# Reading integer phases in order and writing the table in strides: ScalarE's absolute values and sines in an S4D kernel

## The chip, the cores and the metric

The kernel runs on one core of a Trainium2 chip. The metric is the device time of one execution in microseconds (us), the median of several. A profiled execution leaves a trace, which gives the start and the end of each instruction on each engine. TensorE (PE) multiplies matrices, and its weight loads (PEld) are listed by themselves; VectorE (DVE) and ScalarE (ACT) work element by element; GpSimd (POOL) does next to nothing here; SyncE (SP) issues the DMAs.

## The reference

Two layers are computed and laid side by side. Layer A is a Fourier mixing of 2048 x 512 by DFT matrices. Layer B is a diagonal state space convolution: for each of 512 channels d, a kernel of 2048 taps is a sum over 128 states n of exponentials of complex rates, and the input is convolved with it.

```python
dt = jnp.exp(log_dt)
A = -jnp.exp(log_A_real) + 1j * A_imag
C = (C_real + 1j * C_imag) * dt[:, None]
P = jnp.exp((A * dt[:, None])[:, :, None] * pos[None, None, :])
K = 2.0 * jnp.einsum("dn,dnl->dl", C, P).real
...
y = jnp.fft.irfft(jnp.fft.rfft(u_t, L2) * jnp.fft.rfft(K, L2)[None], L2)[:, :, :L]
return y + u * D_skip[None, None, :]
```

The change lies in how the powers P are made: magnitude times cosine and sine of a phase.

## The kernel before, in words

A tap position is split into a coarse and a fine part, so that a tap is a product of two small complex tables, summed over the 128 states by TensorE. The states lie on the partitions. The channels are worked in 16 rounds of CHUNK = 32. In each round two tables are made:

- `t2`, [128, 32 channels d, 2 halves h, 2 parts c (real, imaginary), 32 positions l], of which positions 0 to 19 of each half come from phases. There are two of these tables, used in turn.
- `t1`, [128, 32 channels d, 2 parts c, 32 positions l], also with two buffers.

The phases are 32-bit integers, a full turn being 2^32, so that additions wrap by themselves. `phases2` and `phases1` (VectorE, line 977, from seeds that ScalarE copies in at lines 991, 992 and 1006) build them by doubling in `p2` [128, 40 positions, 32 channels] and `p1` [128, 32 positions, 32 channels]: position is the outer axis and channel the inner one. The tables have it the other way round, channel outside and position inside.

`sines` fills a table from its phases with three ScalarE instructions: the absolute value of the phases into the real part (line 1022), the sine of the phases into the imaginary part (line 1024), and then, in place over the real part, the sine of a quarter turn less the absolute value, which is the cosine (line 1026). The first two have 40 x 32 = 1280 elements on each partition for `t2` and 32 x 32 = 1024 for `t1`; each runs 16 times at each size. Once the sine into the imaginary part is done, the phase buffer may be written again (`p2s`, `p1s`: one buffer of each).

Behind `sines`, `magnitudes2` (product at line 1067) and `magnitudes1` (line 1088) multiply the tables by magnitudes that VectorE grows in `mag`, with the channel outside and the position inside; their seeds are written by ScalarE at lines 1059, 1060 and 1081, one float for each channel. `squares` (lines 1109 to 1120) makes further even positions of `t2` by squaring. `taps` (line 1151) multiplies `t1` by `t2` on TensorE, line 1156 copies the taps out, and line 1177 starts the Fourier transform of the taps. The rest of layer B (lines 1188 to 1411) and layer A (lines 253 to 612) run on the same engines in between.

The order of the instructions on each engine is laid down by a small planner in the program: each step is a generator that names an engine and an estimated duration before it issues its instruction, and `Plan.run` always takes the step that could start first. For the three steps of `sines` the estimate is `act(n) + 0.15` with `n` the product of the table view's extents, and `act(cols)` is `0.09 + cols * 0.00085`. Nothing in the planner knows strides. Memory and results are guarded by semaphores and events (`t1s`, `t2s`, `raw1_ev`, `raw2_ev`).

Of the kernel before, what the change touches and what calls it, by code (L numbers as in the profile page):

```python
# [12 lines left out]
AF = mybir.ActivationFunctionType  # L13
# [8 lines left out]
TWO_PI = 6.283185  # L22
LN2_HI = 0.693359375
LN2_LO = 0.693147180559945309 - LN2_HI
TURN = 2.0 ** 32
# [163 lines left out]
def act(cols):  # L189
    return 0.09 + cols * 0.00085  # L190
# [491 lines left out]
class Ssm:  # L682
# [334 lines left out]
    def sines(self, re, im, p, sign):  # L1017


        a, n = self.nc.scalar, math.prod(re.shape[1:])  # L1020
        yield "act", act(n) + 0.15
        a.activation(re, p, AF.Abs)  # L1022
        yield "act", act(n) + 0.15
        a.activation(im, p, AF.Sin, scale=sign * TWO_PI / TURN)  # L1024
        yield "act", act(n) + 0.15
        a.activation(re, re, AF.Sin, scale=-TWO_PI / TURN, bias=self.halfpi)  # L1026

    def sines2(self, n):
        yield self.t2s
        t, p = self.t2[n % 2], self.p2.rearrange("p (h l) d -> p d h l", h=2)  # L1030
        yield from self.sines(t[:, :, :, 0, :20], t[:, :, :, 1, :20], p, 1.0)
        self.plan.put(self.p2s)
        self.plan.set(self.raw2_ev[n])

    def sines1(self, n):
        yield self.t1s
        t = self.t1[n] = self.tab.tile([128, CHUNK, 2, 32], F32, name="t1", bufs=2)
        yield from self.sines(t[:, :, 0], t[:, :, 1], self.p1.rearrange("p m d -> p d m"), -1.0)
        self.plan.put(self.p1s)
        self.plan.set(self.raw1_ev[n])  # L1040

# [462 lines left out]
```

## Time and profile before

| | us |
|---|---|
| median of 3 runs | 607.92 (607.63 to 609.17) |
| the profiled execution | 607.69 |
| its span, first to last instruction | 605.8 |
| ScalarE busy | 424.0 (70% of the span) |
| TensorE matmuls busy | 430.5 (71%) |
| VectorE busy | 391.3 (65%) |
| line 1022, 32 instructions | 71.2 busy, 2230 ns each |
| line 1024, 32 instructions | 70.5 busy, 2203 ns each |
| line 1026, 32 instructions | 39.6 busy, 1247 ns each |

A row of a group names the line, the engine, the operation, what is written from what, the shape (partitions x elements on each, type) and the count; then busy us in total and the mean ns of one; then the idle time of the engine just before those instructions, with what ended it. A row of the waits reads: who waited, for whom, us in total, how many times, the longest. Of the 605.8 us, the chain that ended last can be followed back only through the last store, so the argument goes by stretches of time and by the waits instead.

### The profile page before, as it was taken

To read this page: it belongs to the slowest core of one execution; us is meant where nothing else is said; L and a number is where in the kernel's file an instruction comes from. 1 tells how busy PE (TensorE), PEld (TensorE's weight loads), DVE (VectorE), ACT (ScalarE), POOL (GpSimd) and SP (SyncE) were. 2 spreads that over 40 slices of the span, in tenths; PEclk is the share of its full clock that TensorE was granted. 3 is DMA by queue.
4 is the path that set the end of the run, shared out by engine and by line. 5 is a ranking of instruction groups with operands and counts; after the bars stand their busy time and mean duration, and the time that the engine had idled before them with its cause. 6 is when DMAs were issued, how large, how long until landed. Compare 5 with 4: busy or idle time off the path is not lost. (4 is left out here: it accounts for less than half of the span.)

```text
span 605.8 us, 13828 instructions
## 1 busy us (share of the span) xinstructions
PE 430.5 (71%) x5602; PEld 208.0 (34%) x5634; DVE 391.3 (65%) x843; ACT 424.0 (70%) x662; POOL 10.9 (2%) x25
## 2 busy tenths in 40 slices
PE   4678923196886967738885969798894887777542
PEld 3122201043332333333332443244243344445532
DVE  4996988656696757969976566589694563233110
ACT  2247488999979698886699697789948973434420
POOL 0000000000010001000001000000000000000000
PEclk7899965698997979959797979799997898788796
DMA  8979874184324692866486776284318137599893
GB/s 318 359 232 311 304 267 140 67 313 149 92 79 138 174 293 67 240 196 206 125 274 208 173 206 204 69 216 143 106 32 214 36 124 209 167 248 243 241 230 84
DMA packets 138837, 113.52 MB, mean 187 GB/s; under 512 B 64401, under 2 KB 108817, under 8 KB 138513
## 3 DMA queue, kind: packets, MB, share of 16 engines
q1 hardware_dynamic: 138048, 111.41, 60.8%
q10 hardware_dynamic: 720, 1.18, 0.5%
q8 instruction: 46, 0.75, 0.5%
q14 instruction: 23, 0.18, 0.1%
HBM read 78.09 MB, written 34.47 MB: 186 GB/s over the span
## 5 line engine op out<-in xcount | busy, mean ns | idle before, releaser
L587 PE MATMUL f<-p,w 128*128 128x512 f32 x128 | 73.8, 661 | 19.8 <-ACT y L612 18.7
L1022 ACT ACTIVATE t<-phase 128x1280 f32<-128x1280 int32 (+1 forms) x32 | 71.2, 2230 | 11.8 <-DVE phase L977 7.4
L1024 ACT ACTIVATE t<-phase 128x1280 f32<-128x1280 int32 (+1 forms) x32 | 70.5, 2203 | 0.1
L1067 DVE TENSOR_TENSOR t<-t,mag 128x2560 f32<-128x2560 f32 x16 | 45.2, 2824 | 36.8 <-ACT t L1026 36.8
L1088 DVE TENSOR_TENSOR t<-t,mag 128x2048 f32<-128x2048 f32 x16 | 36.6, 2290 | 49.7 <-ACT t L1026 49.7
L1046 DVE TENSOR_TENSOR mag<-mag,seeds 128x32 f32<-128x32 f32 (+5 forms) x176 | 61.9, 361 | 2.9 <-ACT mag L1059 2.4
L1151 PE MATMUL taps<-t,t 128*32 128x64 f32 x2048 | 38.4, 242 | 25.5 <-DVE t L1088 24.4
L977 DVE CUSTOM_DVE_ANT_0 phase<-seeds,phase 128x512 uint16<-128x512 uint16 (+4 forms) x128 | 52.8, 417 | 0.5
L1151 PEld LDWEIGHTS taps<-t,t 128*32 128x32 f32 x2048 | 35.6, 125 | 35.6 <-DVE t L1088 13.3
L1238 PE MATMUL f<-big,ib 64*128 64x512 f32 x64 | 21.8, 783 | 34.9 <-ACT big L1247 34.9
L514 PE MATMUL f<-base,es 128*128 128x512 f32 x64 | 38.3, 683 | 10.6 <-ACT xi L273 10.4
L587 PEld LDWEIGHTS f<-p,w 128*128 128x128 f32 x128 | 24.4, 204 | 46.6 <-ACT y L612 23.9
L416 DVE CUSTOM_DVE_ANT_1 rest<-slots,base 128x1024 bf16<-128x1024 f32 (+1 forms) x27 | 36.7, 1358 | 4.6 <-PE third L520 2.4
L1026 ACT ACTIVATE t<-t,halfpi 128x1280 f32<-128x1280 f32 (+1 forms) x32 | 39.6, 1247 | 0.0
L514 PE MATMUL f<-base,ec 128*128 128x512 f32 x64 | 35.9, 643 | 0.6 <-ACT low L567 0.6
L1319 PE MATMUL f<-big,w 64*32 64x256 f32 (+1 forms) x768 | 25.8, 392 | 14.4 <-ACT p L548 5.7
L1177 PE MATMUL f<-ks,f1k 32*128 32x512 f32 x128 | 25.8, 673 | 9.1 <-POOL ks L1166 7.2
L517 PE MATMUL f<-rest,xi 128*128 128x512 bf16 x89 | 27.8, 412 | 6.3 <-DVE small L416 3.3
L517 PE MATMUL f<-rest,xr 128*128 128x512 bf16 x85 | 25.0, 380 | 6.3 <-DVE small L416 5.8
L1335 ACT ACTIVATE big<-f 128x1024 f32<-128x1024 f32 x24 | 23.7, 1010 | 6.9 <-PE f L1319 4.6
L517 PEld LDWEIGHTS <-xr 128*128 128x128 bf16 (+1 forms) x144 | 13.5, 94 | 38.8 <-issue 31.3
L520 PE MATMUL third<-rest,small 128*1 128x512 bf16 x96 | 26.4, 384 | 0.0
(222 smaller groups left out, 766.0 us busy)
## 6 DMA issues: line engine op xcount, KB each, us to landing
slots<-in_sT SPq DMA_DIRECT2D x93, 256.0 KB, 4.6
xu<-big SPq DMA_DIRECT2D x16, 512.0 KB, 4.6
xk<-big SPq DMA_DIRECT2D x32, 256.0 KB, 4.5
base<-in_sT SPq DMA_DIRECT2D x31, 256.0 KB, 4.6
big<-xu SPq DMA_DIRECT2D x20, 256.0 KB, 4.5
big<-xk SPq DMA_DIRECT2D x20, 256.0 KB, 4.8
zs<-mid SPq DMA_DIRECT2D x20, 256.0 KB, 3.0
big<-zs SPq DMA_DIRECT2D x10, 512.0 KB, 6.1
```

Of the source, the lines that this page charges most:

```text
L416: return v.tensor_tensor_reduce(rest[:, lo:hi:step], raw[:, lo:hi:step], base[:, None, :].to_broadcast([128, n, DM]), 1.0, 0.0, op, OP.max ...
L514: nc.tensor.matmul(out, x[:, cols], base, start=k == 0, stop=False)
L517: nc.tensor.matmul(out, still[:, cols], rest[:, h], start=False, stop=k == 3 and h == 2)
L587: nc.tensor.matmul(ps, self.w[k][:, cols], self.p[t, c][:, d], start=k == 0, stop=False)
L977: self.nc.vector.tensor_tensor(p[:, to:to + m], p[:, of:of + m], seed[:, None, :].to_broadcast([128, m, CHUNK]), op=OP.add)
L1022: a.activation(re, p, AF.Abs)
L1024: a.activation(im, p, AF.Sin, scale=sign * TWO_PI / TURN)
L1026: a.activation(re, re, AF.Sin, scale=-TWO_PI / TURN, bias=self.halfpi)
L1046: self.nc.vector.tensor_tensor(p[:, :, to:to + m], p[:, :, of:of + m], seed[:, :, None].to_broadcast([128, CHUNK, m]), op=OP.mult)
L1067: v.tensor_tensor(t, t, p.rearrange("p d (h l) -> p (d h) l", h=2)[:, :, None, :].to_broadcast([128, 2 * CHUNK, 2, 20]), op=OP.mult)
L1088: v.tensor_tensor(t, t, p[:, :, None, :].to_broadcast([128, CHUNK, 2, 32]), op=OP.mult)
L1151: nc.tensor.matmul(ps[32 * j:32 * j + 32, i], t1[:, d, c], t2[:, d, :, c], start=c == 0, stop=c == 1, tile_position=(0, 32 * j))
```

## The change

The two instructions that read phases now walk over the elements in the order in which the phases lie: position outside, channel inside. The read goes through neighbours; the table is addressed through a view with its axes turned, so that each element is written one channel's distance from the last, 128 floats for `t2` and 64 for `t1`. The cosine's instruction keeps the old walk. The values are the same, at the same places.

```diff
         a, n = self.nc.scalar, math.prod(re.shape[1:])
+
+        def turned(x):
+            return x.rearrange("p d h l -> p h l d" if len(x.shape) == 4 else "p d l -> p l d")
         yield "act", act(n) + 0.15
-        a.activation(re, p, AF.Abs)
+        a.activation(turned(re), p, AF.Abs)
         yield "act", act(n) + 0.15
-        a.activation(im, p, AF.Sin, scale=sign * TWO_PI / TURN)
+        a.activation(turned(im), p, AF.Sin, scale=sign * TWO_PI / TURN)
         yield "act", act(n) + 0.15
         a.activation(re, re, AF.Sin, scale=-TWO_PI / TURN, bias=self.halfpi)

     def sines2(self, n):
         yield self.t2s
-        t, p = self.t2[n % 2], self.p2.rearrange("p (h l) d -> p d h l", h=2)
+        t, p = self.t2[n % 2], self.p2.rearrange("p (h l) d -> p h l d", h=2)
         yield from self.sines(t[:, :, :, 0, :20], t[:, :, :, 1, :20], p, 1.0)
...
-        yield from self.sines(t[:, :, 0], t[:, :, 1], self.p1.rearrange("p m d -> p d m"), -1.0)
+        yield from self.sines(t[:, :, 0], t[:, :, 1], self.p1, -1.0)
```

## The prediction

> **What bounds the kernel now.** I read the page first, then the busy time by stretches, then who waits for whom, then the groups of ScalarE kept apart by shape.
>
> The stretches say where the change can act. Columns after the length: busy us and instruction count of PE, PEld, DVE, ACT, POOL, then the granted clock, the DMA share and GB/s.
>
> ```profile
> 0.00:85.00 85.00, 60.29 (x189) 21.42 (x192) 70.26 (x156) 38.17 (x87) 1.33 (x17) 0.89 0.87 298
> 85.00:505.00 420.00, 307.23 (x3792) 141.83 (x3817) 300.70 (x659) 353.93 (x528) 9.30 (x7) 0.88 0.53 161
> 505.00:606.00 101.00, 62.96 (x1624) 44.73 (x1625) 20.32 (x31) 31.94 (x48) 0.23 (x1) 0.82 0.78 203
> L1022 ACT ACTIVATE t<-phase x32: 1896/2240/2533, 85.9 to 496.1; 128x1280 f32<-128x1280 int32 x16, 128x1024 f32<-128x1024 int32 x16
> ```
>
> The last row (one line's instructions: min/median/max ns, first and last start) puts the absolute values between 85.9 and 496.1 us; the sines stand among them. In that middle stretch ScalarE is the fullest engine: 353.9 of 420 us, 84%, against 307 for TensorE's matmuls and 301 for VectorE. Before 85 us and behind 505 us the edited lines do not run.
>
> The waits say who suffers from ScalarE there.
>
> ```profile
> DVE t L1088 <- ACT t L1026: 49.7, 13, 8.3
> DVE t L1067 <- ACT t L1026: 36.8, 12, 7.8
> PE taps L1151 <- DVE t L1088: 24.4, 6, 9.6
> ACT ks L1156 <- PE taps L1151: 15.6, 7, 4.8
> ```
>
> L1026 is the last of the three ScalarE steps that fill a table. VectorE waits 49.7 + 36.8 = 86.5 us for it, TensorE 24.4 us for VectorE's product behind it, and ScalarE's own wait leads back to TensorE's taps. It is one loop through three engines with ScalarE as its slowest member, so a microsecond on ScalarE in this stretch is nearly a microsecond of the kernel. I take the 0.84 by which ScalarE is full as the conversion, 1.0 and 0.5 as its ends.
>
> **The change part by part.** Nothing is added, removed or moved. L1022 and L1024 still touch the same 1280 or 1024 elements of each partition, 32 of each, and the third step (L1026) keeps its pattern. The cost that the plan is given comes from the product of the extents, which turning the axes leaves alone, so every queue, SP's and POOL's too, keeps its order; no wait and no DMA is new. Both lines exchange which side strides. Before, phases are read at 128 bytes a step (32 integers of four bytes) and the table is written in runs of 20 or 32 neighbours. After, phases are read as neighbours and the table is written one float at a time, 512 bytes apart in the large table (2 x 2 x 32 floats), 256 in the small one (2 x 32 floats).
>
> Term 1, what the strided read costs now. These are groups by shape, busy us and mean ns, then idle time before.
>
> ```profile
> L1022 ACT ACTIVATE t<-phase 128x1280 f32<-128x1280 int32 x16 | 39.5, 2466 | 10.2 <-DVE phase L977 5.8 <-PE taps L1151 4.4
> L1024 ACT ACTIVATE t<-phase 128x1280 f32<-128x1280 int32 x16 | 38.8, 2424 | 0.1
> L1022 ACT ACTIVATE t<-phase 128x1024 f32<-128x1024 int32 x16 | 31.9, 1995 | 1.6 <-DVE phase L977 1.6
> L1024 ACT ACTIVATE t<-phase 128x1024 f32<-128x1024 int32 x16 | 31.7, 1981 | 0.0
> L1026 ACT ACTIVATE t<-t,halfpi 128x1280 f32<-128x1280 f32 x16 | 21.6, 1351 | 0.0
> L1110 ACT ACTIVATE square<-t 128x512 f32<-128x512 f32 x16 | 9.9, 621 | 0.0
> L1110 ACT ACTIVATE square<-t 128x256 f32<-128x256 f32 x16 | 6.5, 405 | 0.0
> ```
>
> L1110 walks in runs at two sizes: (621 - 405) / 256 = 0.844 ns an element, and 621 - 512 x 0.844 = 189 ns fixed. The strided reads, with 189 taken off, cost (2466 - 189) / 1280 = 1.78, (2424 - 189) / 1280 = 1.75, 1.76 and 1.75 ns an element: a bit over twice 0.844. L1026 over the same table, in runs, takes 1351, so the 1.1 us above it is the price of the stride.
>
> Term 2, what a strided write costs. The kernel has such writes already, though short: the seeds of the magnitudes go into a table at 160 bytes a step (L1059, L1060: 40 floats) and 128 (L1081: 32 floats), out of neighbours.
>
> ```profile
> L1060 ACT ACTIVATE mag<-seeds 128x64 f32<-128x64 f32 x16 | 5.0, 312 | 0.0
> L1059 ACT ACTIVATE mag<-seeds 128x32 f32<-128x32 f32 x16 | 4.0, 250 | 0.0
> L1081 ACT ACTIVATE mag<-seeds 128x32 f32<-128x32 f32 x16 | 4.0, 248 | 0.2 <-DVE t L1088 0.2
> L992 ACT ACTIVATE phase<-seeds 128x64 int32<-128x64 int32 x16 | 3.9, 242 | 0.0
> L1006 ACT ACTIVATE phase<-seeds 128x32 int32<-128x32 int32 x16 | 3.5, 217 | 0.0
> L933 ACT ACTIVATE seeds<-par 128x64 f32<-128x64 f32 x8 | 2.0, 245 | 0.0
> ```
>
> 64 floats in runs take 245 (L933), 64 strided ones 312; 32 integers in runs take 217 (L1006), 32 strided floats 248 to 250. The extra grows with the count, 31 to 33 ns for 32 and 67 for 64, so it is a price per element and not a fixed one. L992 and L1006 also read integers in runs at (242 - 217) / 32 = 0.78 ns: it is not the type that makes the phases slow. With the 189 off, the strided write costs (312 - 189) / 64 = 1.92, (250 - 189) / 32 = 1.91 and (248 - 189) / 32 = 1.84 ns an element, beside 1.75 to 1.78 for the strided read.
>
> No row writes single floats 256 or 512 bytes apart, so this price is bounded. Upper end: (312 - 250) / 32 = 1.94. Lower end: if a strided write took just twice a write in runs, 2 x 0.844 = 1.69. I take 1.84, that of L1081: its step of 128 bytes is a power of two like the new ones. At 1.84 the large table's steps take 189 + 1280 x 1.84 = 2544 ns, the small one's 189 + 1024 x 1.84 = 2073. Against the rows of term 1 that is +78, +120, +78 and +92 ns, 368 together, and 16 x 368 = +5.9 us of ScalarE. At 1.94 (2672 and 2176) it is 16 x 830 = +13.3 us; at 1.69 (2352 and 1920) 16 x (-322) = -5.2 us.
>
> The Trainium skill, "SBUF — State Buffer" (Specifications, and the note on cachelines), states 16-byte lines that need at least two hits each for full bandwidth, with a penalty for each access that crosses to a new line. It names neither reads nor writes; applied to both, the penalty is moved by this change and not avoided, and the sum would be near zero. The rows agree: 1.75 to 1.78 for reads and 1.84 to 1.92 for writes, where every element meets another line.
>
> Term 3, the tail. ScalarE starts an instruction before the one ahead of it has ended.
>
> ```profile
> 232.33 0.24 ACT L992 ACTIVATE phase<-seeds 128x64 int32<-128x64 int32 x1
> 232.48 1.90 ACT L1335 ACTIVATE big<-f 128x1024 f32<-128x1024 f32 x2
> 235.92 0.31 ACT L1060 ACTIVATE mag<-seeds 128x64 f32<-128x64 f32 x1
> 236.07 0.24 ACT L933 ACTIVATE seeds<-par 128x64 f32<-128x64 f32 x1
> 199.60 2.52 ACT L1024 ACTIVATE t<-phase 128x1280 f32<-128x1280 int32 x1
> 202.03 1.34 ACT L1026 ACTIVATE t<-t,halfpi 128x1280 f32<-128x1280 f32 x1
> ```
>
> (Start, duration.) Behind L992, in runs, the next starts 232.33 + 0.24 - 232.48 = 0.09 us early; behind the strided write of L1060 it is 235.92 + 0.31 - 236.07 = 0.16; behind the strided read of L1024 0.09. The read side is done earlier than the write side, and 0.07 us of the tail lies under the next instruction. I count it once a table, at the step that writes in runs again: 32 x 0.07 = -2.2 us. Its other end is nothing.
>
> Sum on ScalarE: +5.9 - 2.2 = +3.7 us; on the span +3.7 x 0.84 = +3.1. The profiled execution took 607.69 us (span 605.8), 0.23 under the median of 607.92, so the sum gives 610.8; I say 611. Ends: 13.3 without the tail, fully converted, gives 621; -5.2 - 2.2 = -7.4 x 0.84 = -6.2 gives 601. The granted clock of TensorE (0.88 in the middle stretch) I leave as it is, since no matmul is changed.
>
> **The rivals.** B, not slower but much faster: a strided write costs nothing over a run of any length, because the engine hands its results on and goes ahead. For it speaks term 3, where the next instruction starts 0.15 us behind L1060 just as behind L992. Then each step falls to 189 + 0.844 an element, 1269 and 1053 ns: 16 x (1197 + 1155 + 942 + 928) = 67.6 us less on ScalarE. Its busy time in the middle would be 286 us, under TensorE's 307, so late next would be TensorE; between half and 0.84 of 67.6 comes off, 34 to 57 us, say 45: 563 us. Against it: the end of L1060 is 67 ns late for 64 floats, twice what it is for 32, and a store that is behind by 1 ns an element must hold up 1280 of them unless it keeps some hundreds back. It decides from the point at which the store holds more than about half an instruction. Chance 0.13.
>
> The Trainium skill, "ScalarE: Activation LUTs" (What ACT_TABLE_LOAD costs), gives 186 ns + 0.833 ns an element for an instruction with immediate scale and bias, whatever the function; taken to hold as long as the input runs on, it is B's rule, with 1252 ns for 1280 elements. L1110's 0.844 agrees, L1022's 1.78 shows that it does not hold for every pattern.
>
> C, far slower: steps of 256 and 512 bytes meet the same part of the memory each time, which 128 and 160 bytes do not.
>
> ```profile
> L1109 ACT ACTIVATE t<-t 128x256 f32<-128x256 f32 x16 | 6.6, 411 | 5.4 <-DVE t L1120 5.2
> ```
>
> L1109 writes runs of four floats 256 bytes apart into the large table, at 411 ns where L1110, in runs, takes 405. So a step of 256 bytes every four elements costs next to nothing, and a new line cannot take longer than about 4 x 0.844 = 3.4 ns. At that end the steps are 189 + 1280 x 3.38 = 4515 and 3650 ns, 16 x (2049 + 2091 + 1655 + 1669) = +119 us on ScalarE, and the kernel would be near 608 + 119 x 0.9 = 715. Nothing shown speaks for it. Chance 0.05.
>
> D, the price is the same but the loop hides it: ScalarE's 66 idle us in the middle stretch take up the extra, and the kernel stays within 2 us of 608. Against it, its waits there are for results that hang on ScalarE. Chance 0.08, inside my range.
>
> **How the numbers follow.** A measurement of this kernel can tell about 0.3%, 1.8 us, from no change. A, writes at about the price of reads, has 0.82 with D, with the price from 1.69 to 1.94 and the conversion open: 0.17 of it below 606.1, 0.24 within 1.8 us, 0.41 above 609.7. B gives 0.13 to faster, C 0.05 to slower: 0.30, 0.24, 0.46. The range is A's, 601 to 621, one us wider below for the matmuls that fall elsewhere against the clock: 600 to 621. It leaves out B, C and little more.
>
> **What would show it.** L1022 and L1024 at 2.5 us for 1280 and 2.1 for 1024, L1026 unchanged at 1.35, ScalarE at some 357 to 360 us over the middle stretch and the waits for L1026 still at 80 to 95 us: A. L1022 at 1.3 us and VectorE hardly waiting for L1026: B. L1022 above 3 us: C. Wrong on the size alone I would be if the price of a write over a long walk differs from that over 32 and 64 elements, the one step that no row shows.

## The result and the profile after

The changed kernel takes 605.81 us (median of 14 runs) beside 609.17 for the kernel before (14 runs): ratio 0.9939, 95% interval 0.9912 to 0.9966, some 3.7 us (2.1 to 5.4) faster. The forecast was 611 us and slower. The time lies in the range, the sign is wrong. Ratios here and below leave out executions more than 1.5% above their kernel's fastest, and so can differ a little from the quotient of two medians.

In what follows a side of an instruction "runs" where it goes from neighbour to neighbour, and is "strided" where each element lies a step away from the last. "From start to start" is the time from the start of an instruction to that of the next on the same engine.

The page of the profiled execution (605.65 us, span 603.8) and the middle stretch, in the columns used before:

```profile
span 603.8 us, 13828 instructions
PE 433.6 (72%) x5602; PEld 210.6 (35%) x5634; DVE 391.5 (65%) x843; ACT 418.0 (69%) x662; POOL 10.9 (2%) x25
85.00:505.00 420.00, 310.74 (x3831) 143.69 (x3861) 301.76 (x659) 347.71 (x528) 9.30 (x7) 0.88 0.53 162
```

ScalarE is busy for 418.0 us instead of 424.0, with the same 662 instructions; VectorE's 391.5 is that of before. The groups by shape of the three steps, whose lines are now 1025, 1027 and 1029, and behind them the one row of before that the prediction does not show:

```profile
L1025 ACT ACTIVATE t<-phase 128x1280 f32<-128x1280 int32 x16 | 39.3, 2456 | 9.7 <-DVE phase L977 5.3 <-PE taps L1154 4.2
L1027 ACT ACTIVATE t<-phase 128x1280 f32<-128x1280 int32 x16 | 38.7, 2420 | 0.1
L1025 ACT ACTIVATE t<-phase 128x1024 f32<-128x1024 int32 x16 | 32.0, 2000 | 2.5 <-DVE phase L977 2.5
L1027 ACT ACTIVATE t<-phase 128x1024 f32<-128x1024 int32 x16 | 31.7, 1982 | 0.0
L1029 ACT ACTIVATE t<-t,halfpi 128x1280 f32<-128x1280 f32 x16 | 21.3, 1329 | 0.0
L1029 ACT ACTIVATE t<-t,halfpi 128x1024 f32<-128x1024 f32 x16 | 17.8, 1114 | 0.0
L1026 ACT ACTIVATE t<-t,halfpi 128x1024 f32<-128x1024 f32 x16 | 18.3, 1142 | 0.0
```

The mean durations of the edited steps moved by -10, -4, +5 and +1 ns: a strided write costs, over this length, what the strided read cost. The cosine, not edited, is 22 to 28 ns shorter. That explains 0.9 us of ScalarE, and 6.0 are gone. Busy time counts a stretch in which two instructions overlap once, and the rest is seen in no duration but in the starts. The timeline of ScalarE (start, duration), first round, before:

```profile
85.95 2.41 ACT L1022 ACTIVATE t<-phase 128x1280 f32<-128x1280 int32 x1 [0.57 <-DVE phase L977]
88.26 2.38 ACT L1024 ACTIVATE t<-phase 128x1280 f32<-128x1280 int32 x1
90.54 1.35 ACT L1026 ACTIVATE t<-t,halfpi 128x1280 f32<-128x1280 f32 x1
91.79 1.99 ACT L1022 ACTIVATE t<-phase 128x1024 f32<-128x1024 int32 x1
93.69 2.00 ACT L1024 ACTIVATE t<-phase 128x1024 f32<-128x1024 int32 x1
95.59 1.13 ACT L1026 ACTIVATE t<-t,halfpi 128x1024 f32<-128x1024 f32 x1
```

and after:

```profile
85.80 2.44 ACT L1025 ACTIVATE t<-phase 128x1280 f32<-128x1280 int32 x1 [0.58 <-DVE phase L977]
88.01 2.40 ACT L1027 ACTIVATE t<-phase 128x1280 f32<-128x1280 int32 x1
90.19 1.36 ACT L1029 ACTIVATE t<-t,halfpi 128x1280 f32<-128x1280 f32 x1
91.41 2.03 ACT L1025 ACTIVATE t<-phase 128x1024 f32<-128x1024 int32 x1
93.20 2.03 ACT L1027 ACTIVATE t<-phase 128x1024 f32<-128x1024 int32 x1
94.98 1.17 ACT L1029 ACTIVATE t<-t,halfpi 128x1024 f32<-128x1024 f32 x1
```

Before, the sine starts 85.95 + 2.41 - 88.26 = 0.10 us ahead of the end of the absolute value; after, 85.80 + 2.44 - 88.01 = 0.23 us. Over all rounds without a wait between, the next instruction starts 0.10 us early behind a strided read and 0.20 behind a strided write. From the first start to the sixth it is 9.64 us before and 9.18 after: 0.46 us a round, 16 x 0.46 = 7.4 us on ScalarE (7.2 from the means of all rounds).

The kernel got about half of that. ScalarE's idle time (span less busy) went from 181.8 to 185.8 us in these two executions, and the waits show a part of it:

```profile
DVE t L1091 <- ACT t L1029: 46.5, 12, 8.0
DVE t L1070 <- ACT t L1029: 35.4, 12, 7.6
PE taps L1154 <- DVE t L1091: 25.0, 5, 9.3
ACT ks L1159 <- PE taps L1154: 18.7, 6, 6.2
```

VectorE waits 81.9 us for the cosine instead of 86.5; ScalarE's wait for the taps is up from 15.6 to 18.7. (These are waits of the whole execution, as in the prediction's rows; between 85 and 505 us the wait for the taps is 10.8 and 12.5.)

### The profile page after: what moved, and what is told of

Same layout as the page of the kernel before. It is cut to its first block, busy times and chain, and to the rows that moved or that the text cites. A ratio compares the mean times of both kernels' runs of the same rounds, so it can differ in the third digit from the quotient of the medians.

```text
span 603.8 us, 13828 instructions
## 1 busy us (share of the span) xinstructions
PE 433.6 (72%) x5602; PEld 210.6 (35%) x5634; DVE 391.5 (65%) x843; ACT 418.0 (69%) x662; POOL 10.9 (2%) x25
## 5 line engine op out<-in xcount | busy, mean ns | idle before, releaser
L1027 ACT ACTIVATE t<-phase 128x1280 f32<-128x1280 int32 (+1 forms) x32 | 70.4, 2201 | 0.1
L1154 PE MATMUL taps<-t,t 128*32 128x64 f32 x2048 | 40.4, 248 | 26.4 <-DVE t L1091 25.0
L1154 PEld LDWEIGHTS taps<-t,t 128*32 128x32 f32 x2048 | 37.4, 130 | 36.5 <-DVE t L1091 15.1
L1123 DVE TENSOR_TENSOR t<-t,square 128x512 f32<-128x512 f32 (+1 forms) x32 | 17.8, 555 | 14.6 <-ACT square L1113 13.7
```

The source lines that it names most:

```text
L1027: a.activation(turned(im), p, AF.Sin, scale=sign * TWO_PI / TURN)
L1154: nc.tensor.matmul(ps[32 * j:32 * j + 32, i], t1[:, d, c], t2[:, d, :, c], start=c == 0, stop=c == 1, tile_position=(0, 32 * j))
```

## The experiments

Theory T: a strided write lasts as long as a strided read, but ScalarE's next instruction may start 0.1 us earlier behind it; that time is the gain. Rival R: ScalarE's pace is hidden, and the gain comes from other engines or from phases that are freed earlier.

**Give the time back.** The changed kernel, with a small copy behind each edited step:

```diff
         a.activation(turned(re), p, AF.Abs)
+        for _ in range(1):
+            a.activation(self.pad, self.f1k[:, 0, :32], AF.Copy)
...
         a.activation(turned(im), p, AF.Sin, scale=sign * TWO_PI / TURN)
+        for _ in range(1):
+            a.activation(self.pad, self.f1k[:, 0, :32], AF.Copy)
```

> The changed kernel with one small ScalarE copy (32 floats) behind each absolute value and each sine, 64 in all; nothing else differs. Theory T (the gain is ScalarE time: behind a strided write the next instruction starts 0.2 us before the end instead of 0.1): a copy of 32 floats holds ScalarE for 0.12 us, so 64 x 0.12 = 7.7 us come back, ScalarE's busy time is 424 to 427 us, and the kernel stands at that of before, ratio 0.998 to 1.003. Rival R (other engines, or the earlier freeing of the phases, gave the gain; ScalarE's pace is hidden): ratio stays at 0.992 to 0.996.

Measured: ratio to before 1.0036 (1.0007 to 1.0065). The timeline, first round:

```profile
85.50 2.43 ACT L1026 ACTIVATE t<-phase 128x1280 f32<-128x1280 int32 x1 [0.58 <-DVE phase L978]
87.73 0.22 ACT L1028 ACTIVATE pad<-f1k 128x32 f32<-128x32 f32 x1
87.82 2.36 ACT L1030 ACTIVATE t<-phase 128x1280 f32<-128x1280 int32 x1
89.99 0.21 ACT L1032 ACTIVATE pad<-f1k 128x32 f32<-128x32 f32 x1
90.08 1.34 ACT L1034 ACTIVATE t<-t,halfpi 128x1280 f32<-128x1280 f32 x1
```

The copy starts 0.20 us ahead of the end of the step, inside its tail, and the sine 0.09 us behind the copy. So a copy holds ScalarE for 0.09 us and not 0.12: 64 x 0.09 = 5.8 us, and 0.8 more from the cosine, which is back at 1354 and 1142 ns behind a copy. ScalarE is busy for 423.4 us, as before the change. 6.6 us given back cost 1.0036 - 0.9939 = 0.97%, 5.9 us (3.5 to 8.3 by the two intervals). The ratio lies just above the 0.998 to 1.003 expected of T and clear of R's 0.992 to 0.996: ScalarE's pace is not hidden. The copies put the end of the sine back too, so this run alone does not exclude R's other half, phases that are freed earlier. The traces before and after do: no instruction of another engine waits for the sine (L1024, then L1027), and VectorE's waits for the copies of the phases' seeds are the same, 2.7 and 2.5 us. So R falls, and the gain is ScalarE time.

**Each line alone.** Both start from the changed kernel. The first has the absolute value turned and the sine as before, the second the other way round:

```diff
+        def walked(x):
+            return x.rearrange("p h l d -> p d h l" if len(x.shape) == 4 else "p l d -> p d l")
...
-        a.activation(turned(im), p, AF.Sin, scale=sign * TWO_PI / TURN)
+        a.activation(im, walked(p), AF.Sin, scale=sign * TWO_PI / TURN)
```

> Only the absolute value walks in the phases' order; the sine walks as before. T: the absolute value frees ScalarE about 0.10 us earlier (next start 1.80 and 2.24 us behind its own, from 1.89 and 2.35), the sine as before (1.88 and 2.33), the cosine as before (1.04 and 1.25); ScalarE busy about 421 us. R: nothing of this is bound to the one edited line.

> Only the sine walks in the phases' order. T: the sine frees ScalarE about 0.10 us earlier (1.78 and 2.22 us from start to next start, from 1.88 and 2.33), the absolute value as before (1.89 and 2.35); if the cosine's shortening by 0.025 us comes from the strided write just ahead of it, it shows here (1.01 and 1.23) and not where the absolute value alone is turned; ScalarE busy about 420.5 us. R: nothing of this is bound to the one edited line.

One execution of each was taken (609.1 and 605.9 us), which tells nothing where those of the changed kernel lie between 600.6 and 609.4; the traces do. First the absolute value alone, then the sine alone:

```profile
86.82 2.44 ACT L1027 ACTIVATE t<-phase 128x1280 f32<-128x1280 int32 x1 [0.57 <-DVE phase L977]
89.06 2.34 ACT L1029 ACTIVATE t<-phase 128x1280 f32<-128x1280 int32 x1
91.30 1.35 ACT L1031 ACTIVATE t<-t,halfpi 128x1280 f32<-128x1280 f32 x1
```

```profile
85.60 2.40 ACT L1027 ACTIVATE t<-phase 128x1280 f32<-128x1280 int32 x1 [0.57 <-DVE phase L977]
87.89 2.37 ACT L1029 ACTIVATE t<-phase 128x1280 f32<-128x1280 int32 x1
90.06 1.34 ACT L1031 ACTIVATE t<-t,halfpi 128x1280 f32<-128x1280 f32 x1
```

The early start follows the edited line: 0.20 and 0.10 us in the first, 0.11 and 0.20 in the second. Means over all rounds from start to start are 2.24 and 2.31 against 2.35 and 2.22 us at 1280 elements. The cosine is 1354 ns with the absolute value alone turned and 1330 with the sine alone: its 25 ns go with the strided write just ahead of it. ScalarE is busy for 421.1 and 420.0 us, as expected.

**Both sides strided.** In the changed kernel, the small table alone is walked so that neighbours on neither side follow each other:

```diff
-            return x.rearrange("p d h l -> p h l d" if len(x.shape) == 4 else "p d l -> p l d")
+            if len(x.shape) == 4:
+                return x.rearrange("p d h l -> p h l d")
+            return x.rearrange("p d (g l) -> p l d g", l=4)
...
-        yield from self.sines(t[:, :, 0], t[:, :, 1], self.p1, -1.0)
+        yield from self.sines(t[:, :, 0], t[:, :, 1], self.p1.rearrange("p (g l) d -> p l d g", l=4), -1.0)
```

> The changed kernel, with the small table walked so that both sides step: reads 512 bytes, writes 16 bytes a step, each element in another line on both sides; the large table as in the changed kernel. T (the two sides work side by side, and the early start behind a strided write comes from the read side finishing ahead of the write side): the two steps of 1024 still last about 2.0 us, and since the read side is no longer ahead the next start is again 0.1 us before the end (1.88 to 1.90 us from start to start). Rival (the two prices add): 189 + 1024 x 2.6 = 2.85 us. Rival (the early start belongs to strided writes as such): 2.0 us and a start 0.2 us before the end.

Groups by shape and the first round of the small table, from the one execution (603.9 us):

```profile
L1027 ACT ACTIVATE t<-phase 128x1024 f32<-128x1024 int32 x16 | 32.8, 2052 | 1.6 <-DVE phase L977 1.6
L1029 ACT ACTIVATE t<-phase 128x1024 f32<-128x1024 int32 x16 | 32.4, 2026 | 0.0
```

```profile
91.24 2.08 ACT L1027 ACTIVATE t<-phase 128x1024 f32<-128x1024 int32 x1
93.16 2.06 ACT L1029 ACTIVATE t<-phase 128x1024 f32<-128x1024 int32 x1
95.08 1.13 ACT L1031 ACTIVATE t<-t,halfpi 128x1024 f32<-128x1024 f32 x1
```

The two prices do not add (2.05 us, not 2.85), and the start is again about as late as with a strided read: 1.92 and 1.90 us from start to start on the mean of all rounds (1.89 and 1.88 before, 1.80 and 1.78 in the changed kernel), 0.12 to 0.14 early on the mean. The cosine behind them takes 1139 ns again, beside 1142 before and 1114 in the changed kernel. So neither the early start nor the shorter cosine belongs to strided writes as such. That the early start needs a read side that is ahead of the write side, and that the engine keeps some results back for the slower write side, fits all of this but is not shown: the run also shortened the step of the write, from 256 to 16 bytes, and the store itself was not measured.

**Runs on both sides.** From the kernel before; phases are read in the order in which they lie and the table is written in its own:

```diff
-        t, p = self.t2[n % 2], self.p2.rearrange("p (h l) d -> p d h l", h=2)
+        t, p = self.t2[n % 2], self.p2.rearrange("p m d -> p (m d)").rearrange("p (d h l) -> p d h l", h=2, l=20)
...
-        yield from self.sines(t[:, :, 0], t[:, :, 1], self.p1.rearrange("p m d -> p d m"), -1.0)
+        yield from self.sines(t[:, :, 0], t[:, :, 1], self.p1.rearrange("p m d -> p (m d)").rearrange("p (d m) -> p d m", m=32), -1.0)
```

> The kernel before, with the phases read in the order in which they lie and the table written in the order in which it lies; phases land at other places of the table, so the tables hold the wrong taps. Both T and the prediction's case B: 1269 and 1053 ns for the two steps at the two sizes, 67 us less on ScalarE. T, by the share of the ScalarE time that the change gave to the kernel (about 7 us of ScalarE, 3.7 of the kernel): 0.5 x 67 = 34 us, ratio 0.944. The conversion of the prediction, 0.84: 57 us, ratio 0.907. R: ScalarE's pace is hidden, ratio over 0.98.

Measured: 545.12 us, ratio 0.892 (0.8877 to 0.8962). The absolute value and the sine take 1268 and 1261 ns at 1280 elements, 1046 and 1044 at 1024, as the prediction's case B had them for this pattern:

```profile
L1022 ACT ACTIVATE t<-phase 128x1280 f32<-128x1280 int32 x16 | 20.3, 1268 | 11.3 <-DVE phase L977 6.3 <-PE taps L1151 4.9
L1022 ACT ACTIVATE t<-phase 128x1024 f32<-128x1024 int32 x16 | 16.7, 1046 | 3.3 <-DVE phase L977 3.3
```

Start to start that is 67 us less on ScalarE, and the kernel is 10.8%, 66 us, faster. Both conversions in the expectation were too low. But not all of the 66 us need be ScalarE's: TensorE's granted clock, as a share of full speed, was 0.90 in the profiled execution against 0.87 before, and its matmuls were busy for 422.6 us against 430.5.

**Three copies instead of one.** The first experiment's edit, with 3 for 1.

> The changed kernel with three small ScalarE copies behind each absolute value and each sine, 192 in all: 192 x 0.12 = 23 us more on ScalarE than the changed kernel, 16 more than before. If a microsecond of ScalarE is worth 0.77 to 1 us of the kernel, as between the changed kernel and the one with 64 copies (0.98 % for 7.7 us) and the one with runs on both sides: 18 to 23 us over the changed kernel, ratio to before 1.024 to 1.032. If it is worth only 0.5 (3.7 us for 7.2): 12 us over it, ratio 1.013.

Measured: ratio 1.0625 (1.0574 to 1.0675), far above what was expected. The copies of a group do not overlap, as a single copy overlaps its neighbours; probably they wait for each other because they write the same tile (copies to separate tiles were not run):

```profile
227.36 0.75 ACT L1028 ACTIVATE pad<-f1k 128x32 f32<-128x32 f32 x3
228.02 0.40 ACT L1117 ACTIVATE t<-t 128x256 f32<-128x256 f32 x1
```

A group of three holds ScalarE for 0.66 us, 64 of them for 42. Over the changed kernel the time is 1.0625 - 0.9939 = 6.9% longer, 42 us. In the two profiled executions ScalarE's busy time is up from 418.0 to 454.3 us and the time from 605.65 to 642.55, 36 and 37 us. The dose was mistaken, the conversion is again near 1.

**Phases in pairs.** From the kernel before, with another layout: positions 2g and 2g + 1 of a channel lie side by side in the phases, so that the read goes pair by pair and the table is written in runs. The seeds of the integer additions have to be doubled for it:

```diff
-        self.p1, self.p2 = (tab.tile([128, m, CHUNK], I32, name=f"phase{m}") for m in (32, 40))
+        self.p1, self.p2 = (tab.tile([128, m // 2, CHUNK, 2], I32, name=f"phase{m}") for m in (32, 40))
+        self.twice = [tab.tile([128, 4, CHUNK, 2], I32, name=f"twice{m}") for m in range(4)]
...
+            twice = self.twice[n % 2]
+            a.activation(twice, s[:, 2:6, :, None].to_broadcast([128, 4, CHUNK, 2]), AF.Copy)
...
-        t, p = self.t2[n % 2], self.p2.rearrange("p (h l) d -> p d h l", h=2)
-        yield from self.sines(t[:, :, :, 0, :20], t[:, :, :, 1, :20], p, 1.0)
+        t, p = self.t2[n % 2], self.p2.rearrange("p (h g) d l -> p d h g l", h=2)
+        re, im = (t[:, :, :, c, :20].rearrange("p d h (g l) -> p d h g l", l=2) for c in range(2))
+        yield from self.sines(re, im, p, 1.0)
```

> The kernel before with another layout of the phases: two neighbouring positions of a channel lie side by side, so that the table's order reads pairs of integers (8 bytes) and writes runs. VectorE's additions go on over the same counts; their seeds are doubled by 32 ScalarE copies of 256 integers (about 0.31 us from start to start), and one more short copy a round: 12 us more on ScalarE. If one access for each line is what costs and two in a line are enough: 1270 and 1050 ns for absolute value and sine, 67 - 12 = 55 us less on ScalarE and, at the 0.97 by which the run with runs on both sides turned ScalarE time into time, ratio 0.91 to 0.92. Rival: any step over 4 bytes costs: 2460 and 1990 ns as before, 12 us more, ratio 1.01 to 1.02.

Measured: ratio 0.9129 (0.908 to 0.9178). The doubling steps changed the planner's order, and in it one staged block of layer B's input was written over by another, so the input that this version convolves is wrong; the second version hands the two slots out from a list:

```diff
-        self.xus, free = Sem(2), Sem(2)
+        self.xus, free = (Ring([t[:, k] for k in range(2)]) for t in (self.xu_sb, u_sb))
...
-        x = self.xu_sb[:, m % 2]
+        x = yield from self.xus.take()
```

> The layout in pairs once more, with the two staging slots of layer B's input handed out from a list instead of by the parity of a counter; in the run before, the other order of the steps let one block be staged over another. No count and no size changes against that run: absolute value and sine at 1330 and 1100 ns, ScalarE busy 372 to 376 us, ratio 0.905 to 0.92. Rival: the gain of that run hung on the overwritten block, and the ratio goes back towards 1.

Measured: 555.47 us, ratio 0.9103 (0.9062 to 0.9144). This version beats both kernels by about 9%. Its page and groups by shape:

```profile
PE 422.2 (76%) x5634; PEld 204.1 (37%) x5634; DVE 391.7 (71%) x843; ACT 373.4 (67%) x710; POOL 10.0 (2%) x25
L1039 ACT ACTIVATE t<-phase 128x1280 f32<-128x1280 int32 x16 | 21.4, 1335 | 6.5 <-DVE phase L986 6.1 <-DVE small L464 0.4
L1041 ACT ACTIVATE t<-phase 128x1024 f32<-128x1024 int32 x16 | 17.5, 1093 | 0.0
L1023 ACT ACTIVATE twice<-seeds 128x256 int32<-128x256 int32 x16 | 6.4, 402 | 0.0
```

Two integers side by side are nearly enough: (1335 - 189) / 1280 = 0.90 ns an element, where single steps cost 1.78 and runs 0.84. The first expectation had 1270 and 1050 ns a step, as for runs; the steps take some 5% more. ScalarE is busy for 50.6 us less than before, and the kernel takes 9.0%, some 54.5 us, less; VectorE's busy time is unchanged. Here too TensorE's granted clock was higher, 0.90 against 0.87.

The Trainium skill, "SBUF — State Buffer" (the note on cachelines), asks for two hits in each 16-byte line; by that rule pairs of four bytes run at full pace. The trace nearly agrees: 0.90 ns is 6% above the 0.84 of runs.

## Why the prediction was wrong

- What bounds the kernel: right. ScalarE's time in the middle stretch is the kernel's time; 66 us for 67, 42 for 42 and 54.5 for 50.6 show a conversion near 1, above the 0.84 that was used. Part of these large differences can be TensorE's: its granted clock went with them, 0.90 in the two faster kernels, 0.86 with three copies, 0.87 before, and the runs do not separate the two. For the change itself the conversion was lower: 3.7 us (2.1 to 5.4) for 7.2, about half, with a clock of 0.875 after and 0.870 before. In the two profiled executions ScalarE waits 4 us longer, part of it for TensorE's taps; why a small gain is returned by half and a large one is not stays open.
- Term 1, the strided read's price: right, and unchanged in every kernel that has it. Against runs it is 2466 - 1268 = 1.2 us at 1280 elements and not 1.1: L1026, which it was set against, takes some 85 ns more than the other two steps do in runs.
- Term 2, the strided write's price: right in kind, wrong in size. It was set at 1.84 ns an element, +5.9 us of ScalarE; it is (2456 - 189) / 1280 = 1.77 and (2420 - 189) / 1280 = 1.74, the read's own, and the term is -0.1 us: 16 x (-10 - 4 + 5 + 1) ns. The 1.84 came from L1081, with 32 elements. At 1.76 an element its 248 ns would hold 192 fixed instead of 189: a reading of this kind spreads three nanoseconds over 32 elements and then counts them 1280 times. That the fixed part differs by so much is worked out and not measured.
- Term 3, the tail: the overlap was read correctly off L1060, and mis-sized. It was counted at 0.07 us once a table, at the step that writes in runs again, -2.2 us; the absolute value, whose strided write is followed by another, was given nothing, and no row supported that. It is 0.10 us at each of the 64 steps, and 0.025 more at each cosine: together with term 2, -7.2 us.
- The step that failed is the size of these two terms. Their sum on ScalarE is about -7 us from start to start (-6.0 in busy time) instead of +3.7. Term 2 is off by 6 us and term 3 by 5, and either one put right by itself would have turned the sign: -0.1 - 2.2, or +5.9 - 7.1. That the time fell inside the range is no merit of the forecast, since the range covered both signs.
- Rival B, writes that cost nothing: the long writes hold the engine back as its counter-argument had it. What was in favour of it, the early start, is real, and worth 0.1 us an instruction at 1280 and at 1024 elements, 0.07 at the 64 of L1060. Rival C, 256 and 512 bytes as a worse step: no trace of it. D, the loop that hides ScalarE's time, did not show in full, since with the gain of ScalarE the kernel moved; about half of the gain was hidden.
- The signs that were named for case A, 2.5 and 2.1 us a step and waits of 80 to 95 us for L1026, came as described, and fit the result as well as the forecast; L1026, named as unchanged at 1.35 us, took 1.33. Of ScalarE's busy time, 357 to 360 us were named for the middle stretch and 347.7 came. Start to start would have been the sign to name.

## What to carry to other kernels

In this kernel, moving a stride from the read to the write left its price where it was; a layout that puts two 4-byte elements side by side on the read, with the write in runs, took nearly all of it away. That was worth 9%, the move 0.6%. Add up an in-order engine by the time from start to next start, not by mean durations; here 0.1 us of overlap at 64 places was as much as a few per cent on the longest instructions. Do not carry a price from rows of 32 or 64 elements to 1280 without a second look at the fixed part.

## What the runs showed of the hardware

ScalarE starts its next instruction 0.10 us before the end behind runs and strided reads, 0.20 behind a strided write out of a read in runs, and 0.12 to 0.14 where both sides stride; a cosine lasts 25 ns less right behind the strided write out of runs, and as long as before behind the step with both sides strided (1139 and 1142 ns at 1024 elements). The two sides' prices do not add: 2.05 us for 1024 elements with both strided, 2.00 with either, 1.05 with neither.

The Trainium skill, "ScalarE: Activation LUTs" (What ACT_TABLE_LOAD costs), gives an overlap of about 93 ns between ACTIVATEs that follow each other. The trace agrees behind runs (0.095 us in the kernel with runs on both sides), and shows about twice that behind strided writes.
